# Regrouping the second half of batch 0's attention, and copying the second head group's keys in two parts

## The chip, the cores and the metric

The kernel runs on one core of a Trainium2 chip. The metric is the device time of one execution in microseconds (us), smaller is better. TensorE (PE in the profile, PEld its weight loads), VectorE (DVE), ScalarE (ACT) and GpSimd (POOL) each run their own list of instructions in order; SyncE (SP) only issues transfers. They meet through semaphores.

## The reference

Sigmoid attention over 8 batches, 12 heads, 448 positions and head size 64, followed by a gated feed-forward layer (ReGLU) on the 3584 tokens, model width 768, inner width 1536:

```python
scores = scale * np.matmul(q, k.transpose(0, 1, 3, 2)) - np.log(S)
attn = 1.0 / (1.0 + np.exp(-scores))
x = np.matmul(attn, v)                # then heads are put side by side: 3584 x 768
out = (np.maximum(x @ w_gate, 0.0) * (x @ w_val)) @ w_out
```

## The kernel before

Every instruction stands where the code puts it: the order on each engine is written by hand. The work of a batch goes through these steps.

- **Transposes.** `pe_transposes` (L195) turns the keys or queries of a group of four heads, chunk by chunk (7 chunks of 64 positions), with TensorE (L201) into a PSUM bank `trt`, and one VectorE copy (L206) brings them to `qkT` in SBUF. Keys and queries each take 14 transposes for all 7 chunks.
- **Scores and sigmoid.** In batch 0 the queries are handled in two parts, chunks 0 to 3 (256 columns) and 4 to 6 (192 columns); `FirstSlot` (L263) is one group (three groups) with one part of the queries, so there are six slots: 0 to 2 for the first part, 3 to 5 for the second. A slot has four units: units 0 to 2 hold two key chunks (8 score products, L232, four of them side by side in the array as 64x64 tiles), unit 3 one (4 products). A unit writes a tile of the pool `pairp`, which has two buffers (L69), and one sigmoid on ScalarE (L187) reads it into a `PT` tile. So a unit's products must wait until the sigmoid of the unit before last has read its buffer.
- **Value product.** `pv` (L242) multiplies all pieces of a slot by the values (28 products, L250, 64x64 tiles) into two PSUM banks, and two VectorE instructions (L184) scale them into `xT`.
- **Feed-forward unit.** `gv` (L304) makes, for 128 of the 1536 inner columns, 6 gate products and 6 value products (L309, full 128x128 weights); one instruction takes the maximum with 0 (on VectorE, L320, for the first part of batch 0; on ScalarE, L318, otherwise) and VectorE multiplies (L327). `ffn_mix(n)` (L651) runs the next n of these units. Their banks, those of `trt`, of `pv` and of `keep_warm` are given out in a ring of four (`bank`, L76).
- **Output.** The products with `w_out` follow from batch 2 on, in a form that saves multiplications.

`keep_warm` (L172) issues products of zeros. Loads are issued by GpSimd (L110 to L148) in a fixed order: keys, queries, values, then the weights in pieces of two to three units.

The order of batch 0 is a loop over the six slots and four units (L704); the dictionary `after` (L683) says what follows the unit (slot, unit): the transposes of later groups between slots 0 and 3, the value product of slot i about one slot later, and feed-forward units (first part, inner blocks 0 to 5, pushed at L669) between units of slots 3 to 5. `slots[5].pv()` (L709) ends batch 0's attention; the first call for batch 1 is L780, which transposes batch 1's first group and runs a feed-forward unit of the second part.

Of the kernel before, what the change touches and what calls it, by code (L numbers as in the profile page):

```python
# [17 lines left out]
def kernel(  # L18
# [17 lines left out]
    NCH = S // 64  # L36
# [3 lines left out]
    QCUT = 4  # L40
# [40 lines left out]
    def bank16(name):  # L81
        return bank(name, (P, 1024), FP16)
# [38 lines left out]
    KCUT = 4  # L121
# [50 lines left out]
    def keep_warm(count):  # L172
        ps = bank("warm_ps")
        for _ in range(count):
            nc.tensor.matmul(ps[:, 0:S], zeros[:, 0:P], zeros[:], start=True, stop=True)  # L175
# [14 lines left out]
    def qkT_of(b, g):  # L190
        if (b, g) not in qkT_tiles:
            qkT_tiles[(b, g)] = qkTp.tile([P, TW, P], FP16, tag="qkT", name="qkT")
        return qkT_tiles[(b, g)]

    def pe_transposes(b, g, ti, c0=0, c1=NCH):  # L195
        t16 = in_tiles[b][ti]
        qkT = qkT_of(b, g)
        trt = bank16("trt")
        for c in range(c0, c1):
            for h in range(2):  # L200
                nc.tensor.transpose(  # L201
                    trt[64 * h : 64 * h + 64, c * P : (c + 1) * P],
                    t16[:, 2 * g + h, c * D : (c + 1) * D],
                    ident[:],
                )
        nc.vector.tensor_copy(  # L206
            qkT[:, ti * NCH + c0 : ti * NCH + c1, :].rearrange("p c x -> p (c x)"),
            trt[:, c0 * P : c1 * P],
        )
# [437 lines left out]
    def push_first(half, fs, act_relu=True):  # L647
        c0, c1 = HALVES[half]
        push_gv(0, 64 * c0, 64 * (c1 - c0), fs, act_relu)

    def ffn_mix(count, hooks=()):  # L651
        hooks = list(hooks)
        for left in range(count, -1, -1):
            while hooks and hooks[0][0] >= left:
                hooks.pop(0)[1]()
            if left:
                gv_queue.popleft()()
# [10 lines left out]
    slots = [FirstSlot(half * NG + g, g, half) for half in range(2) for g in range(NG)]  # L668
# [2 lines left out]
        for g in range(1, NG):  # L671
            pe_transposes(0, g, 1, QCUT, NCH)

    def pv_then_ffn(i):
        slots[i].pv()
        ffn_mix(1)

    def ffn_then_pv(i):
        ffn_mix(1)
        slots[i].pv()  # L680


    after = {  # L683
        (0, 0): lambda: pe_transposes(0, 0, 0, KCUT, NCH),
        (0, 1): lambda: keep_warm(2),
        (0, 2): lambda: pe_transposes(0, 1, 0),
        (0, 3): lambda: pe_transposes(0, 1, 1, 0, QCUT),
        (1, 0): lambda: keep_warm(2),
        (1, 1): lambda: pe_transposes(0, 2, 0),
        (1, 2): lambda: pe_transposes(0, 2, 1, 0, QCUT),  # L690
# [5 lines left out]
        (3, 1): slots[2].pv,  # L696
        (3, 2): second_queries,
        (3, 3): lambda: ffn_mix(1),
        (4, 1): lambda: ffn_then_pv(3),
        (4, 3): lambda: ffn_mix(2),  # L700
        (5, 1): lambda: pv_then_ffn(4),
        (5, 3): lambda: ffn_mix(1),
    }
    for i, slot in enumerate(slots):  # L704
        for u in range(4):
            slot.unit(u)
            if (i, u) in after:
                after[(i, u)]()
    slots[5].pv()  # L709
    push_first(1, range(0, 6))  # L710
    for f0 in range(6, 12, 2):
        for half in range(2):
# [188 lines left out]
```

## Time and profile before

| what | value |
|---|---|
| median of 3 runs | 393.63 us (393.59 to 393.73) |
| profiled execution: its time | 393.45 us |
| profiled execution: span from first to last instruction | 391.7 us |
| granted TensorE clock | 1.00 |
| TensorE busy in 5.00 to 10.90 us | 5.37 us |
| TensorE, ScalarE busy in 10.90 to 17.70 us | 6.54, 6.71 us |
| TensorE, ScalarE, VectorE busy in 20.97 to 33.45 us | 12.48, 5.74, 7.64 us |

The span leaves 1.75 us of the execution's own time outside. In the page, a group line gives a line of the kernel, an engine, an operation, the tiles written and read, and how often it runs; the timeline gives the start, the duration and the form of instructions, with neighbours of one kind merged; the chain of waits goes back from the last instruction to whatever released each step. A product's duration includes its way through the array, so the rows of neighbouring products overlap, and TensorE can appear busy while nothing new can start: the distance between starts tells more than the duration.

### The profile page before, as it was taken

Reading aid. Unit: us, or ns where it says so; the run is one execution under the profiler, and the core shown is the slowest. Engines: PE = TensorE matmul, PEld = TensorE weight load, DVE = VectorE, ACT = ScalarE, POOL = GpSimd, SP = SyncE. Lnnn points to the kernel's source line nnn. Section 1 sums busy time; section 2 is a strip of 40 time slices with the busy share of each in tenths; the row PEclk is TensorE's granted clock in tenths of the full one; section 3 lists DMA queues with packets and bytes.
Section 4 is the critical chain, followed back from the end, with each engine's and each line's share of the span. In section 5 each row is a group of like instructions: output and inputs, shape, how many; then the busy total and the mean of one; then the engine's idle time right before and its main releaser. Section 6 shows DMA issues by size and latency. Waiting matters only on the chain.

```text
span 391.7 us, 8761 instructions
## 1 busy us (share of the span) xinstructions
PE 385.1 (98%) x3488; PEld 215.2 (55%) x3488; DVE 282.9 (72%) x556; ACT 226.7 (58%) x480; POOL 49.5 (13%) x73
## 2 busy tenths in 40 slices
PE   8999999999999999999999999999999999999996
PEld 4678786445455545454555554545455555555653
DVE  2464344358388789999757789999967788999563
ACT  4956778784877755555547774545477244333322
POOL 9634310500030300003000300000000000000000
PEclk9999999999999999999999999999999999999999
DMA  9999999998899892225945695133012330000335
GB/s 151 198 200 204 204 202 139 151 203 143 181 164 196 162 216 35 47 49 72 178 99 130 122 196 102 34 48 60 4 30 53 82 80 2 0 1 2 80 87 157
DMA packets 68953, 43.69 MB, mean 112 GB/s; under 512 B 35888, under 2 KB 65584, under 8 KB 68912
## 3 DMA queue, kind: packets, MB, share of 16 engines
q0 software_dynamic: 30736, 23.33, 39.6%
q1 hardware_dynamic: 37664, 19.24, 24.2%
q10 hardware_dynamic: 512, 0.56, 0.5%
q8 instruction: 27, 0.44, 0.4%
q14 instruction: 14, 0.11, 0.1%
HBM read 47.19 MB, written 11.01 MB: 149 GB/s over the span
## 4 chain that ended last, share of the span: by engine, by line
PE 95%; ACT 3%; DVE 1%; issue 0%; ACTq 0%
PE u L385 33%; PE g L385 16%; PE y L385 10%; PE qk_ps L232 9%; PE g_ps L309 8%; PE pv_ps L250 7%; PE v_ps L309 7%; ACT PT L187 2%; PE ya L346 1%; PE warm_ps L175 1%; PE trt L201 1%; PE yb L346 1%; DVE xT L184 0%; DVE qkT L206 0%; DVE S L376 0%
## 5 line engine op out<-in xcount | busy, mean ns | idle before, releaser
L187 ACT ACTIVATE PT<-qk_ps 128x448 f16<-128x448 f32 (+3 forms) x318 | 150.9, 589 | 76.2 <-PE qk_ps L232 76.1
L385 PEld LDWEIGHTS <-S 128*128 128x128 f16 x558 | 54.6, 98 | 45.5 <-issue 0.9
L597 DVE TENSOR_TENSOR gsb<-g,gsb 128x448 f32<-128x448 f32 x72 | 42.9, 625 | 10.4 <-PE g L385 10.0
L232 PE MATMUL qk_ps<-qkT 64*64 64x448 f16 (+2 forms) x756 | 47.4, 335 | 0.8 <-DVE qkT L206 0.5
L385 PEld LDWEIGHTS <-hT 128*128 128x128 f16 x306 | 28.6, 98 | 22.4 <-issue 5.0
L327 DVE TENSOR_TENSOR hT<-gate_sb,v_ps 128x256 f16<-128x256 f32 (+2 forms) x36 | 16.2, 465 | 34.0 <-ACT gate_sb L318 18.0
L593 ACT COPY gsb<-u 128x448 f32<-128x448 f32 x48 | 25.6, 558 | 24.0 <-PE u L385 22.9
L436 ACT ACTIVATE ysb<-u 128x384 f32<-128x384 f32 x31 | 15.3, 492 | 39.4 <-PE u L385 35.2
L184 DVE TENSOR_SCALAR xT<-pv_ps 128x448 f16<-128x448 f32 (+2 forms) x53 | 27.9, 566 | 13.1 <-PE pv_ps L250 12.2
L250 PE MATMUL pv_ps<-PT,v 64*64 64x448 f16 (+2 forms) x756 | 36.6, 329 | 0.0
L309 PE MATMUL g_ps<-xT,wg 128*128 128x256 f16 (+2 forms) x216 | 33.5, 291 | 0.1
L309 PE MATMUL v_ps<-xT,wv 128*128 128x256 f16 (+2 forms) x216 | 33.3, 290 | 0.0
L385 PEld LDWEIGHTS <-wg 128*128 128x128 f16 x216 | 20.2, 98 | 21.8 <-issue 4.3
L385 PEld LDWEIGHTS <-wv 128*128 128x128 f16 x216 | 21.1, 98 | 19.7
L232 PEld LDWEIGHTS <-qkT 64*64 64x64 f16 x756 | 17.9, 105 | 22.0 <-issue 13.8
L454 DVE SCALAR_TENSOR_TENSOR ysb<-y,ysb 128x384 f32<-128x384 f32 x28 | 15.6, 556 | 17.7 <-PE y L385 10.2
L250 PEld LDWEIGHTS <-v 64*64 64x64 f16 x756 | 21.7, 107 | 10.8 <-issue 0.9
L385 PE MATMUL u<-T,hT 128*128 128x384 f16 x138 | 26.2, 326 | 0.0
L309 PEld LDWEIGHTS <-wg 128*128 128x128 f16 x216 | 18.5, 98 | 11.7 <-issue 5.1
L110 POOL DMA_DIRECT2D k<-in_k_dram x14 | 10.9, 776 | 109.2 <-DVE rel L215 102.8
L309 PEld LDWEIGHTS <-wv 128*128 128x128 f16 x216 | 20.2, 98 | 7.4
L385 PE MATMUL u<-xT,wg 128*128 128x448 f16 x108 | 23.5, 354 | 0.0
(76 smaller groups left out, 531.7 us busy)
## 6 DMA issues: line engine op xcount, KB each, us to landing
out_dram<-ysb SPq DMA_DIRECT2D x52, 192.0 KB, 2.9
k<-in_k_dram POOLq DMA_DIRECT2D x5, 672.0 KB, 11.7
q<-in_q_dram POOLq DMA_DIRECT2D x5, 672.0 KB, 14.4
v<-in_v_dram POOLq DMA_DIRECT2D x8, 336.0 KB, 14.5
v<-in_v_dram POOLq DMA_DIRECT2D x16, 168.0 KB, 13.9
k<-in_k_dram POOLq DMA_DIRECT2D x8, 224.0 KB, 11.9
wo<-in_moe_w_out_dram POOLq DMA_DIRECT2D x1, 1536.0 KB, 11.1
q<-in_q_dram POOLq DMA_DIRECT2D x6, 224.0 KB, 12.2
```

The source lines that it names most:

```text
L110: nc.gpsimd.dma_start(t16[:, xs, cs], rows_of(src, b)[:, xs, cs])
L184: nc.vector.tensor_scalar(out=xT, in0=src, scalar1=XSCALE, scalar2=None, op0=AOP.mult)
L187: nc.scalar.activation(PT_ap, ps_ap, AF.Sigmoid, bias=sig_bias, scale=qk_scale)
L232: nc.tensor.matmul(out_of(hh)[o : o + 64, :], qkT[rows, c, cols], qkT[rows, NCH + c0 : NCH + c1, cols], start=True, stop=True, tile_positi ...
L250: nc.tensor.matmul(ps[hh][64 * r : 64 * r + 64, 0:qn], v16[rows, 2 * g + hh, c * D : (c + 1) * D], pieces[c][rows, hh, :], start=(c == 0), ...
L309: nc.tensor.matmul(ps[-1][:, 0:qn], wt[:, dc, f * P : (f + 1) * P], xT_tiles[b][:, dc, q0 : q0 + qn], start=(dc == 0), stop=(dc == NDC - 1),)
L327: nc.vector.tensor_tensor(out=hT_tiles[g][:, f, o : o + qn], in0=gate_sb[:, 0:qn], in1=ps[1][:, 0:qn], op=AOP.mult,)
L385: nc.tensor.matmul(ps[:, 0:n], A[:, k_, :], W[:, k_, :], start=(first and k_ == 0), stop=(k_ == kn - 1), skip_group_check=True,)
L436: nc.scalar.activation(o, ps[:, 0:HM], AF.Copy, scale=OUT_SCALE)
L454: nc.vector.scalar_tensor_tensor(out=o, in0=ps[:, 0:HM], scalar=OUT_SCALE, in1=o, op0=AOP.mult, op1=AOP.add)
L593: by(gs[u][i][:], ps[u][:, 0:S])
L597: nc.vector.tensor_tensor(out=gs[u][i][:], in0=ps[u][:, 0:S], in1=gs[u][i][:], op=AOP.add)
```

## The change

Two edits in the dictionary of batch 0; no instruction other than one VectorE copy is added or taken away.

1. The keys of the second group (g = 1) are transposed in two parts, chunks 0 to 3 with a copy of 512 elements a partition and chunks 4 to 6 with one of 384, where one copy of 896 stood. After unit 2 of slot 0 come the first part of the keys and the queries' chunks 0 to 3 (8 and 8 transposes); the second part of the keys (6) follows unit 3.
2. Slots 4 and 5 no longer have a feed-forward unit between their units: unit 0, unit 1, the value product of the slot before, unit 2 and unit 3 stand together, and two feed-forward units follow. The value product of slot 5, which stood at the end, is put ahead of the last of the six feed-forward units.

```diff
-    def pv_then_ffn(i):
-        slots[i].pv()
-        ffn_mix(1)
+    def first_of_second_group():
+        pe_transposes(0, 1, 0, 0, KCUT)
+        pe_transposes(0, 1, 1, 0, QCUT)
+
+    def last_value_product():
+        ffn_mix(2)
+        slots[5].pv()
+        ffn_mix(1)
-
-    def ffn_then_pv(i):
-        ffn_mix(1)
-        slots[i].pv()
...
-        (0, 2): lambda: pe_transposes(0, 1, 0),
-        (0, 3): lambda: pe_transposes(0, 1, 1, 0, QCUT),
+        (0, 2): first_of_second_group,
+        (0, 3): lambda: pe_transposes(0, 1, 0, KCUT, NCH),
...
-        (4, 1): lambda: ffn_then_pv(3),
+        (4, 1): slots[3].pv,
         (4, 3): lambda: ffn_mix(2),
-        (5, 1): lambda: pv_then_ffn(4),
-        (5, 3): lambda: ffn_mix(1),
+        (5, 1): slots[4].pv,
+        (5, 3): last_value_product,
...
-    slots[5].pv()
```

With u for a unit, P for a value product, F for a feed-forward unit and T for batch 1's transposes, TensorE's order from slot 4 on:

```
before  4u0 4u1 F P3 4u2 4u3 F F 5u0 5u1 P4 F 5u2 5u3 F P5 T
after   4u0 4u1 P3 4u2 4u3 F F 5u0 5u1 P4 5u2 5u3 F F P5 F T
```

## Prediction

> **What bounds the kernel now.** I read the page's engine lines first: TensorE is busy for 98% of the span. Then the chain of waits from 8.6 us on, which tells where the start of the kernel is set:
>
> ```profile
> 8.77 0.53 PE trt L201 x14
> 9.30 0.02 issue
> 9.33 0.62 DVE qkT L206
> 9.95 0.01 issue
> 9.97 0.44 DVE qkT L206
> 10.40 0.04 issue
> 10.45 0.44 PE qk_ps L232 x8
> 10.89 0.02 issue
> 10.91 3.35 ACT PT L187 x4
> 14.26 0.02 issue
> 14.28 3.35 ACT PT L187 x4
> 17.63 0.04 issue
> 17.67 0.36 PE qk_ps L232 x8
> ```
>
> Columns: start, length, who. Up to 10.45 us the two copies of the second group set the pace, then ScalarE's sigmoids without a hole until 17.63, and from 17.67 on the chain has nothing but TensorE for 36 us. So a gain ahead of 17.67 counts only if ScalarE gets it, and behind it each idle stretch of TensorE is lost time. The third view is TensorE's timeline in the stretch that the second edit reorders:
>
> ```profile
> 20.97 0.52 PE L232 MATMUL qk_ps<-qkT 64*64 64x192 f16 x16
> 21.43 0.83 PE L309 MATMUL g_ps<-xT,wg 128*128 128x256 f16 x6
> 22.09 0.82 PE L309 MATMUL v_ps<-xT,wv 128*128 128x256 f16 x6
> 22.84 0.77 PE L250 MATMUL pv_ps<-PT,v 64*64 64x192 f16 x28
> 23.44 0.42 PE L232 MATMUL qk_ps<-qkT 64*64 64x192 f16 x12
> ```
>
> and ScalarE's beside it, one sigmoid a line:
>
> ```profile
> 21.44 0.81 ACT L187 ACTIVATE PT<-qk_ps 128x768 f16<-128x768 f32 x1 [1.17 <-PE qk_ps L232]
> 22.15 0.81 ACT L187 ACTIVATE PT<-qk_ps 128x768 f16<-128x768 f32 x1
> ```
>
> To see: units 0 and 1 of slot 4 start at 20.97; their sigmoids end at 22.25 and 22.96. Units 2 and 3 need the buffers these two read. Today they come at 23.44, because a feed-forward unit and a value product stand between: the wait is there, and hidden.
>
> **Edit 1, the keys in two parts.** Eight transposes take 0.41 and fourteen 0.58 us (rows of the third group, 12.47 and 11.62), so six more cost 0.17. The first key copy can start at 9.33 - 0.17 = 9.16. A copy of 512 takes 0.43 (two in 0.85 at 5.68): it ends at 9.59. The queries' eight transposes follow 8 x 0.028 = 0.23 behind the keys', so their data are there at 9.39 and the second copy runs 9.59 to 10.01, where it ended at 10.39. Keys and queries have landed: the transfers issued at 2.29 and 3.00 took 4.9 and 4.8 us.
>
> Slot 1's unit 0 could start at 10.05 for 10.45. But its buffer is read by the sigmoid of slot 0's unit 2, 9.11 + 1.03 = 10.14, and 0.05 later the products start (13.82 after 13.76 one slot on): 10.19. From products to sigmoid it is 0.46 today (10.45 to 10.91), so 10.65, and ScalarE is free at 10.01 + 0.62 = 10.63. **ScalarE's hole of 0.28 shrinks to 0.02: -0.26 us**, and since its line then has no hole until 17.63, all of it reaches 17.67. The second part's six transposes take the place of the queries' eight, and its copy (0.36, the 384 row at 7.57) runs 10.01 to 10.37, while its first reader, slot 1's unit 2, stands at 12.13. VectorE works 0.17 us more, into idle time (1.85 us ahead of the copy at 12.24). The ring gives out one bank more; its reader of four turns ago is the copy that ended at 7.93. The term lies between -0.28, the whole hole, and 0, if another wait fills it; a loss would need the third copy to hold slot 1's unit 2, and it has 1.8 us of margin.
>
> What is late next: the first unit F starts at 19.30 for 19.56. Its value weights, issued at 9.72, land 9.8 later, at 19.5, and are read at 20.11 - 0.26 = 19.85. That margin of 0.3 holds. Later weights have more, since in the new order unit F number 2 comes 2 us later. GpSimd's and SyncE's lists keep their order, and no transfer moves past another.
>
> **Edit 2, what goes.** Changing between 64x64 and 128x128 products costs TensorE time. An F (a feed-forward unit) that another F follows lasts 1.32 from start to start (23.79 to 25.11), one that a value product follows 1.41 (21.43 to 22.84); the starts unrounded differ by 0.095. **A change is 0.095 us.** From slot 4's unit 0 to the F behind batch 1's transposes (20.97 to 32.36) there are 10 changes today and 7 after. Three fewer: **-0.29 us**.
>
> **Edit 2, what comes.** The new order puts units 2 and 3 right behind the value product. TensorE takes its list in order, so the two F queued behind them wait too, and behind these the next slot. Counting from unit 0's start at 20.97:
>
> - Units 0 and 1 with a value product last 1.03 up to the next F (26.52 to 27.55), less the change 0.095: TensorE is at unit 2 at 21.91. Its buffer is free when unit 0's sigmoid ends, 22.25, plus 0.05: 22.30. Idle 0.39.
> - Unit 2 takes two groups of four, 0.083 each (28.96 to 29.34 is three groups, the start 0.025 and a change): TensorE is at unit 3 at 22.47. Its buffer is free at 22.96 + 0.05 = 23.01. Idle 0.54.
> - Unit 3 to F is 0.21 (19.35 to 19.56): F at 23.22 instead of 22.29.
>
> That is **0.93 to 0.96 us idle in each of the two slots**; slot 5 stands the same way, since its ScalarE line is free when it begins (2.6 us of F lie between). I take 0.95. Units 2 and 3 have no cheaper way out: ScalarE issues its sigmoids 0.71 apart (21.44, 22.15) whatever TensorE does.
>
> **Sum.** 2 x 0.95 - 0.29 = +1.61. By pieces: each slot's attention has 1.50 today (0.46 + 0.095 + 0.95 in slot 4) and 2.25 after (20.97 to 23.22), which is 2 x 0.75, and slot 5's value product ahead of an F adds one change, 0.095: +1.59; with the starts unrounded it is +1.57, which I take. With edit 1: 1.57 - 0.26 = **+1.31 us**. Behind it, batch 1's first score products are reached 1.3 us later, with all inputs ready (its keys and queries landed at 28.8 and 29.9; the copies at 32.15 are no longer queued behind the scaling of slot 5's value product). The profiled execution would go from 393.45 to 394.76 (span 391.7 to 393.0); the median stands 0.18 above that execution, so 393.63 + 1.31 = **394.9 us**. About 0.2% (0.8 us) is what a measurement of this kernel can tell from no change.
>
> **A rule that speaks against the change.** After TensorE's 0.52 us of idle time before 10.45, the next pair of zero products still took 0.55 us, as before it (7.80 and 10.79), with the granted clock at 1.00; so one such hole did not slow it. The Trainium skill, TensorE: Matmul & The Clock Gate, section "A second HAM failure mode: psum-queue depth-cycling", says that short idle times between groups while PSUM buffers are cycled can throw the array back to half clock. The new order makes four holes of that size in 6 us. By the row this costs nothing, by the rule perhaps one window of 3.4 us at half clock, an estimate of 1.7 us from that page.
>
> **The rivals.**
>
> - *A, not slower: units 2 and 3 don't wait.* The mechanism is ScalarE's sigmoid of unit 0 ending before TensorE reaches unit 2, 0.94 us after the slot's start; the point is a sigmoid of 0.42 us. Then the sum is -0.29 - 0.26 = -0.55: 393.1 us. For it: TensorE shows no hole in this stretch today, and slot 3 passes its value product without one at 18.6. Against it: the rows give 0.81, and slot 3's unit 1 was itself held 0.27 us for its buffer (17.40 to 17.67).
> - *B, later waits take the lateness up.* TensorE waits once more behind batch 0's end, 0.68 us for VectorE at 298.57, and the chain goes over ScalarE for 0.54 at 53.77. If both were independent of TensorE: 394.9 - 0.68 - 0.23 = 394.0 (0.23 is what starts lost at 54.35). Against it: both wait for engines that work on TensorE's own results, so they move with it.
> - *C, edit 1 gives nothing,* a landing or a copy taking the hole's place: +1.57, 395.2.
> - *D, the clock falls back.* The trace has half-rate products only in the first 6 us (ten zero products in 3.92 us at 1.16, 0.37 apart, against two in 0.55 later, 0.20 apart), so the price is between 0 and 2.9 us (half of 1.16 to 6.9), 394.9 to 397.8; the nearest row, the hole at 10.45, says 0, and a case of its own begins above 395.4.
>
> **How the numbers follow.** Forecast 0.71, C 0.12, B 0.07, A 0.06, D 0.04. The range 394.4 to 395.4 takes in the forecast with 0.2 either way for the idle time (two slots, 0.1 each), and C: 0.83. Slower by over 0.2% (above 394.42): forecast, C, D, 0.87. Within: B and most of A, 0.11. Faster: 0.02.
>
> **What would show it.** ScalarE's row at 10.91 moves to 10.65 and the hole before it goes. In slots 4 and 5 the score products of units 2 and 3 stand apart, about 1.33 and 2.04 us after unit 0, released by ScalarE; the chain gets ScalarE pieces between 21 and 28 us where it has TensorE alone now. The transposes of batch 1 start at 32.7 for 31.45 and everything behind is 1.3 us later. If units 2 and 3 follow the value product without a hole, or the sigmoids are shorter, the forecast is wrong.

## The result, and the profile after

| | before | after |
|---|---|---|
| median | 393.61 us (393.39 to 393.76, 8 runs) | 394.84 us (394.35 to 395.49, 8 runs) |
| profiled execution: time | 393.45 us | 395.12 us |
| profiled execution: span | 391.7 us | 393.3 us |
| batch 1's first transposes start | 31.45 us | 32.83 us |

The change makes the kernel slower: the medians differ by 1.23 us, and the ratio is 1.0029, 95% interval 1.002 to 1.0039 (0.8 to 1.5 us). The forecast was 394.9.

The page of after first, engines and granted clock:

```profile
PE 385.6 (98%) x3488; PEld 215.6 (55%) x3488; DVE 283.1 (72%) x557; ACT 226.8 (58%) x480; POOL 49.5 (13%) x73
PEclk9999999999999999999999999999999999999999
```

VectorE has one instruction more, everything else the same number, and no slice of the span shows a lower clock. The busy time of TensorE is 98% here as before, and tells nothing of the 1.6 us that the span grew by. The chain of waits of after does (start, length, who):

```profile
8.38 2.32 ACT PT L187 x3
10.70 0.02 issue
10.72 3.35 ACT PT L187 x4
...
17.48 0.36 PE qk_ps L232 x8
...
21.30 0.49 PE pv_ps L250 x23
21.80 0.57 issue
22.37 0.32 PE pv_ps L250 x5
...
26.92 0.81 ACT PT L187
...
27.78 0.28 PE qk_ps L232 x4
```

Two things are to be seen. The copies of the second group have left the chain, and ScalarE leads from 8.38 to 17.44 without a hole: edit 1 does what it says, and TensorE takes over at 17.48 for 17.67. Behind 21 us two pieces have come in that before did not have: a ScalarE piece in slot 5, which was forecast, and an "issue" piece of 0.57 us in the middle of slot 4's value product, which was not. TensorE's timeline of after shows the same two places (the bracket gives the idle time before the row and what ended it):

```profile
20.78 0.53 PE L232 MATMUL qk_ps<-qkT 64*64 64x192 f16 x16
21.13 0.67 PE L250 MATMUL pv_ps<-PT,v 64*64 64x192 f16 x23
22.37 0.32 PE L250 MATMUL pv_ps<-PT,v 64*64 64x192 f16 x5 [0.57 <-issue]
...
23.02 0.83 PE L309 MATMUL g_ps<-xT,wg 128*128 128x256 f16 x6
...
25.74 0.53 PE L232 MATMUL qk_ps<-qkT 64*64 64x192 f16 x16
...
27.07 0.36 PE L232 MATMUL qk_ps<-qkT 64*64 64x192 f16 x8 [0.23 <-ACT PT L187]
27.78 0.28 PE L232 MATMUL qk_ps<-qkT 64*64 64x192 f16 x4 [0.34 <-ACT PT L187]
27.98 0.83 PE L309 MATMUL g_ps<-xT,wg 128*128 128x256 f16 x6
```

From unit 0 to the next feed-forward unit it is 23.02 - 20.78 = 2.24 us in slot 4 and 27.98 - 25.74 = 2.24 in slot 5, where the forecast had 2.25 for each. In slot 5 units 2 and 3 stand 1.33 and 2.04 us after unit 0, each released by ScalarE, to the hundredth as forecast. In slot 4 the time is the same and the place is another: the value product itself stops behind its 23rd product.

Along the program, after against before: slot 4's unit 0 -0.19 us, batch 1's first transposes +1.37, the same until 127 us, where the first score products of a batch wait for a DMA transpose and start 0.16 us later than at before's pace (+1.54 from there on), and +1.6 at the end.

### The profile page after: what moved, and what is told of

Its sections match the earlier page's. It is cut to its first block, busy times and chain, and to the rows that moved or that the text cites. A ratio compares the mean times of both kernels' runs of the same rounds, so it can differ in the third digit from the quotient of the medians.

```text
span 393.3 us, 8762 instructions
## 1 busy us (share of the span) xinstructions
PE 385.6 (98%) x3488; PEld 215.6 (55%) x3488; DVE 283.1 (72%) x557; ACT 226.8 (58%) x480; POOL 49.5 (13%) x73
## 4 chain that ended last, share of the span: by engine, by line
PE 92%; ACT 4%; DMA 1%; DVE 1%; issue 0%; ACTq 0%
PE u L385 32%; PE g L385 16%; PE y L385 9%; PE qk_ps L232 9%; PE g_ps L309 8%; PE pv_ps L250 8%; PE v_ps L309 7%; ACT PT L187 3%; DMA qkT<-rel 1%; PE ya L346 1%; PE warm_ps L175 1%; PE trt L201 1%; PE yb L346 1%; DVE xT L184 0%; DVE S L376 0%
## 5 line engine op out<-in xcount | busy, mean ns | idle before, releaser
L232 PE MATMUL qk_ps<-qkT 64*64 64x448 f16 (+2 forms) x756 | 47.8, 336 | 1.3 <-ACT PT L187 0.9
L309 PE MATMUL g_ps<-xT,wg 128*128 128x256 f16 (+2 forms) x216 | 33.5, 291 | 0.1
L309 PE MATMUL v_ps<-xT,wv 128*128 128x256 f16 (+2 forms) x216 | 33.3, 290 | 0.0
L385 PEld LDWEIGHTS <-wg 128*128 128x128 f16 x216 | 20.2, 98 | 21.8 <-issue 4.3
L232 PEld LDWEIGHTS <-qkT 64*64 64x64 f16 x756 | 18.2, 106 | 22.8 <-issue 14.5
L250 PEld LDWEIGHTS <-v 64*64 64x64 f16 x756 | 21.8, 107 | 11.4 <-issue 1.5
L385 PE MATMUL u<-T,hT 128*128 128x384 f16 x138 | 26.3, 326 | 0.0
L309 PEld LDWEIGHTS <-wg 128*128 128x128 f16 x216 | 18.6, 98 | 11.4 <-issue 5.1
L309 PEld LDWEIGHTS <-wv 128*128 128x128 f16 x216 | 20.2, 98 | 7.4
```

The costliest lines, as they stand in the source:

```text
L232: nc.tensor.matmul(out_of(hh)[o : o + 64, :], qkT[rows, c, cols], qkT[rows, NCH + c0 : NCH + c1, cols], start=True, stop=True, tile_positi ...
L250: nc.tensor.matmul(ps[hh][64 * r : 64 * r + 64, 0:qn], v16[rows, 2 * g + hh, c * D : (c + 1) * D], pieces[c][rows, hh, :], start=(c == 0), ...
L309: nc.tensor.matmul(ps[-1][:, 0:qn], wt[:, dc, f * P : (f + 1) * P], xT_tiles[b][:, dc, q0 : q0 + qn], start=(dc == 0), stop=(dc == NDC - 1),)
L385: nc.tensor.matmul(ps[:, 0:n], A[:, k_, :], W[:, k_, :], start=(first and k_ == 0), stop=(k_ == kn - 1), skip_group_check=True,)
```

## The experiments

Times are medians, each against runs of the kernel before taken beside it, with the ratio's 95% interval. In the traces the start of slot 0 moves by up to 0.6 us from one execution to the next, and it is the earlier the sooner the record of the full clock begins (4.6 to 7.0 us); places are therefore given as "relative", from slot 0's first score product. Batch 1's first score product stands at 26.63 relative in before and 27.97 in after.

**Edit 1 alone.**

```diff
...
-        (0, 2): lambda: pe_transposes(0, 1, 0),
-        (0, 3): lambda: pe_transposes(0, 1, 1, 0, QCUT),
+        (0, 2): first_of_second_group,
+        (0, 3): lambda: pe_transposes(0, 1, 0, KCUT, NCH),
```

> The kernel before with edit 1 alone (the second group's keys in two parts). Theory: the hole of 0.28 us in front of ScalarE's row at 10.91 shrinks to about 0.02 and all of it reaches the end: 393.61 - 0.26 = 393.35 us. Rival (the hole's place is taken by another wait, or ScalarE's gain is lost behind 17.67): 393.6 us.

Measured: 393.69 against 393.68, ratio 1.0002 (0.9993 to 1.0011). By itself the edit shows no gain. In the trace its 0.26 us are there in slot 1 and in slot 4 (each 0.26 earlier, relative) and gone at batch 1 (26.64 relative). TensorE's timeline of this kernel shows where, and its list of waits says for what (engine, line, releaser: us in total, times, longest):

```profile
27.06 0.83 PE L309 MATMUL g_ps<-xT,wg 128*128 128x256 f16 x6
27.98 0.83 PE L309 MATMUL v_ps<-xT,wv 128*128 128x256 f16 x6
```

```profile
PEld L309 <- DMA wv<-in_moe_w_val_dram: 0.4, 1, 0.4
```

Gate to value products takes 0.66 us elsewhere and 0.92 here: the value weights of inner blocks 4 and 5 land at 27.93. The DMA engines are busy for 90% or more of this stretch (every slice from 9 to 30 us shows 9 in the DMA row), so an earlier reader only waits longer. How much it waits changes with the execution: in before the same weights landed at 27.56, 0.65 us ahead of their reader, and in the second trace of before (the last experiment) at 27.92, only 0.06 ahead. This trace also loses 0.32 us at 126 us to a DMA transpose.

**Edit 2 alone.**

```diff
...
-        (4, 1): lambda: ffn_then_pv(3),
+        (4, 1): slots[3].pv,
         (4, 3): lambda: ffn_mix(2),
-        (5, 1): lambda: pv_then_ffn(4),
-        (5, 3): lambda: ffn_mix(1),
+        (5, 1): slots[4].pv,
+        (5, 3): last_value_product,
...
-    slots[5].pv()
```

> The kernel before with edit 2 alone (slots 4 and 5 unbroken, slot 5's value product ahead of the last feed-forward unit). Theory: two slots with units 2 and 3 held for ScalarE, 2 x 0.95 us idle, three changes of the array's form fewer: 393.61 + 1.57 = 395.2 us, with the holes in front of units 2 and 3. Rival (the loss comes from the two edits together, for example a transfer that is reached too early): between 393.6 and 394.5 us.

Measured: 394.79 against 393.68, ratio 1.0031 (1.0019 to 1.0044): +1.11 us (0.75 to 1.73) for a theory of +1.57; in the trace batch 1 stands 1.7 us later, relative. Edit 2 alone loses as much as the whole change, within the intervals. TensorE's timeline:

```profile
20.81 0.52 PE L232 MATMUL qk_ps<-qkT 64*64 64x192 f16 x16
...
22.64 0.32 PE L250 MATMUL pv_ps<-PT,v 64*64 64x192 f16 x5 [0.82 <-issue]
...
23.15 0.83 PE L309 MATMUL g_ps<-xT,wg 128*128 128x256 f16 x6
```

Slot 4 lasts 2.34 us to its feed-forward unit, 0.1 more than the sigmoids ask for, and the hole is again behind the 23rd product. No semaphore ends it: "issue" means that the profile shows nothing that TensorE waited for.

**After, with short sigmoids in slots 4 and 5.**

```diff
             n = qn * len(cs)
-            sigmoid(PT[:, :, 0:n], ps[:, :, 0:n])
+            m = qn if self.number > 3 else n
+            if m < n:
+                nc.vector.memset(PT[:, :, m:n], 0.0)
+            sigmoid(PT[:, :, 0:m], ps[:, :, 0:m])
```

> The changed kernel, but in slots 4 and 5 the sigmoids of units 0 to 2 take only the first of their two chunks, and VectorE sets the other half of the tile to zero: that part of the attention is left out, the products all stay. Theory (units 2 and 3 wait for the sigmoids of units 0 and 1): a sigmoid of 0.49 instead of 0.81 us lets unit 2 start 1.01 and unit 3 1.41 us after unit 0, and the next feed-forward unit 1.62 instead of 2.24: 0.62 less in each slot, 394.84 - 1.24 = 393.6 us. Rival (TensorE's holes come from its own instruction supply or the clock, not from ScalarE): 394.8 us.

Measured: 393.88 against 393.68, ratio 1.0011 (1.0002 to 1.002); 0.96 us under after. TensorE's timeline, slot 4 and slot 5 (L309 of the other kernels is L312 here):

```profile
20.39 0.53 PE L232 MATMUL qk_ps<-qkT 64*64 64x192 f16 x16
...
21.86 0.32 PE L250 MATMUL pv_ps<-PT,v 64*64 64x192 f16 x5 [0.45 <-issue]
...
22.36 0.83 PE L312 MATMUL g_ps<-xT,wg 128*128 128x256 f16 x6
...
25.09 0.53 PE L232 MATMUL qk_ps<-qkT 64*64 64x192 f16 x16
...
26.10 0.66 PE L232 MATMUL qk_ps<-qkT 64*64 64x192 f16 x12
26.69 0.83 PE L312 MATMUL g_ps<-xT,wg 128*128 128x256 f16 x6
```

Slot 5 falls from 2.24 to 1.60 us and its ScalarE holes are gone: there the sigmoids were the cause. They still set the pace, since units 2 and 3 start at 26.10 and 26.48, each 0.05 us after a sigmoid's end (26.05 and 26.43). Slot 4 falls only to 1.97, because the hole behind the 23rd product stays. So slot 4 has two limits that end close together.

**Slot 4 alone regrouped.**

```diff
-        (4, 1): lambda: ffn_then_pv(3),
-        (4, 3): lambda: ffn_mix(2),
+        (4, 1): slots[3].pv,
+        (4, 3): lambda: ffn_mix(3),
```

> The kernel before with slot 4 alone unbroken (its feed-forward unit stands behind unit 3, so three follow there); slot 5 as before. Theory: half of the regrouping's cost, 2.25 us for 1.50 in slot 4: 393.61 + 0.75 = 394.35 us. Rival (only slot 5, or the place of the last value product, costs): 393.6 us.

Measured: 394.08 against 393.68, ratio 1.0011 (1.0002 to 1.002). The trace has the hole at its longest, 1.04 us, with slot 4 starting early (20.59) and needing 2.57 us to its feed-forward unit:

```profile
22.66 0.32 PE L250 MATMUL pv_ps<-PT,v 64*64 64x192 f16 x5 [1.04 <-issue]
```

The end of the hole doesn't follow the start of slot 4: 22.37 in after (slot 4 from 20.78), 22.64 in edit 2 alone (20.81), 22.66 here (20.59), 21.86 with short sigmoids (20.39).

**After, with four zero products fewer ahead of slot 4.**

```diff
-        (1, 3): lambda: keep_warm(2),
-        (2, 0): lambda: keep_warm(2),
```

> The changed kernel without the four zero products that follow unit 3 of slot 1 and unit 0 of slot 2. In all four kernels with slot 4 unbroken so far TensorE stopped behind the same product, number 351 of its list, which is the 23rd of slot 4's value product, about 1.5 us after a packet of the instruction queue had ended. If TensorE's list arrives in blocks and the hole is the wait for the next one, it stands again behind product 351, now the 27th of the value product. If the hole belongs to the value product (its pieces or banks), it stands behind the 23rd again. The time tells little: 394.8 us by both.

Measured: 395.36 against 393.85, ratio 1.0042 (1.0028 to 1.0056). TensorE's timeline:

```profile
20.73 0.75 PE L250 MATMUL pv_ps<-PT,v 64*64 64x192 f16 x27
22.41 0.24 PE L250 MATMUL pv_ps<-PT,v 64*64 64x192 f16 x1 [0.93 <-issue]
```

Four products fewer ahead, and the hole stands four products later, behind the 27th. It belongs to a place in TensorE's list, behind its 351st product, and not to a tile or a buffer. The page's row of the instruction queue gives packets, MB and the share of the DMA engines:

```profile
q8 instruction: 27, 0.44, 0.4%
```

That is some 16 KB for each packet, and in each of the five kernels with this hole (after, edit 2 alone and the last three above) one packet ends 1.46 to 1.65 us before the hole does. In before, TensorE reaches product 351 at 23.04, 1.73 us after the packet's end at 21.31: no hole, by a margin of 0.1 to 0.3 us. The median is 0.5 us above the forecast: slot 4 lasts 2.45 us here for 2.24 in after, and score products at 100 and 127 us start 0.26 and 0.10 us later than at before's pace, behind DMA transposes.

**Slot 5 alone regrouped.**

```diff
-        (5, 1): lambda: pv_then_ffn(4),
-        (5, 3): lambda: ffn_mix(1),
+        (5, 1): slots[4].pv,
+        (5, 3): lambda: ffn_mix(2),
```

> The kernel before with slot 5 alone unbroken (its feed-forward unit stands behind unit 3, two there); slot 4 as before. Theory: ScalarE's two holes alone, without a hole of TensorE's list, F 2.24 us after unit 0, and 2.24 for 1.50: 393.68 + 0.74 = 394.4 us. Rival (the slot's cost was that of the list's blocks): 393.7 us.

Measured: 394.2 against 393.85, ratio 1.001 (1.0001 to 1.0019). The trace has the forecast's two holes and nothing else in slot 5. The first row below is slot 4's value product, which is that of before:

```profile
22.85 0.91 PE L250 MATMUL pv_ps<-PT,v 64*64 64x192 f16 x28
...
28.00 0.36 PE L232 MATMUL qk_ps<-qkT 64*64 64x192 f16 x8 [0.23 <-ACT PT L187]
28.70 0.28 PE L232 MATMUL qk_ps<-qkT 64*64 64x192 f16 x4 [0.34 <-ACT PT L187]
28.91 0.83 PE L309 MATMUL g_ps<-xT,wg 128*128 128x256 f16 x6
```

Slot 5's unit 0 starts at 26.66, so it is 2.25 us to the feed-forward unit; and from slot 5's unit 0 to batch 1's first score product 7.67 us for 6.93: +0.74, as expected. The value product of slot 4 takes 0.91 us for 0.77 in before: product 352 starts 0.14 us behind product 351, 1.60 us after a packet's end (21.59). So the list can hold TensorE without any change ahead of that place; no gap shows, because the row of the product before lasts 0.24 us. The medians of this and of slot 4 alone (+0.35 and +0.40) are about half of the +0.75 that each was expected to cost, which lies at the upper edge of both intervals, and lower than the traces' local sums (+0.74 and +1.05). In both profiled executions the clock came up early (5.3 and 4.6 us for 6.7 in before), which starts slot 0 0.4 to 0.5 us sooner. Whether that is so in the timed runs is not shown, so the split of the 1.1 us between the slots stays open within the intervals (0.0 to 0.8 us each).

**Edit 1 with the value weights in smaller pieces.** Does edit 1 pay if its new wait is taken away?

```diff
-    load_gv(4, 6)
+    load_gv(4, 5)
+    load_gv(5, 6)
```

> Edit 1 alone, with the weights of inner blocks 4 and 5 loaded one block at a time (four transfers for two). Edit 1 alone gained 0.26 us up to slot 5 and lost it in front of the value half of block 4, whose weights landed at 27.93. Theory: the value weights of block 4 alone land about 1 us sooner, that wait goes, and edit 1's gain reaches the end: 393.68 - 0.26 = 393.4 us. Rival (the smaller transfers cost the saturated queue as much as they bring, or a later landing takes the place): 393.7 us.

Measured: 394.18 against 393.85, ratio 1.0013 (1.0004 to 1.0021). The value weights of block 4 now land at 26.09, the wait is gone, and batch 1 starts 0.25 us earlier than in before (26.38 relative). In this trace it is lost one batch on, as the chain of waits and TensorE's timeline show (L233 is the other kernels' L232):

```profile
54.31 8.58 DMA qkT<-rel
```

```profile
62.93 0.57 PE L233 MATMUL qk_ps<-qkT 64*64 64x448 f16 x8 [0.77 <-DMA qkT<-rel]
```

A DMA transpose of 8.58 us holds batch 2's first score products until 62.93, 0.84 us later than at before's pace. The median is 0.33 us above before, where 0.26 below was expected, so edit 1's gain isn't seen in the time of this kernel either.

**One feed-forward unit in every gap, on top of edit 1.** The opposite of edit 2: cover between units instead of grouping.

```diff
     def pv_then_ffn(i):
         slots[i].pv()
+        ffn_mix(2)
+
+    def transposes_then_pv():
+        pe_transposes(1, 0, 0)
+        pe_transposes(1, 0, 1)
+        slots[5].pv()
         ffn_mix(1)
...
-        (4, 3): lambda: ffn_mix(2),
+        (4, 3): lambda: ffn_mix(1),
...
-        (5, 3): lambda: ffn_mix(1),
+        (5, 3): transposes_then_pv,
...
-    slots[5].pv()
...
-    ffn_mix(1, [(1, lambda: both(1, 0))])
+    ffn_mix(1)
```

> Edit 1, and every place where a unit's products would wait for ScalarE keeps a feed-forward unit: slot 4 as before but one such unit behind it instead of two, two behind slot 4's value product, and batch 1's transposes between slot 5's unit 3 and its value product, so that they cover the sigmoids there; one feed-forward unit follows. Value half of inner block 4 comes 1.3 us later in the order, so its weights' landing holds nothing. Theory: ScalarE's hole goes (0.26) and one change of the array's form (0.095), with no hole of ScalarE's in slots 4 and 5: the first product of batch 1 stands 26.3 us after slot 0's first for 26.63 before, and the time is 0.35 below the kernel before. Rival (the next limit, TensorE's list or a landing, takes it back): no difference, the first product of batch 1 at 26.6.

Measured: 394.0 against 393.88, ratio 1.0004 (0.9996 to 1.0013): no difference, and batch 1's first score product stands at 27.13 relative, 0.5 us behind before, where 26.3 was expected. TensorE no longer waits for ScalarE in slots 4 and 5; it waits for the loads instead. TensorE's timeline, one of the two places:

```profile
29.99 0.58 PE L201 MATMUL trt<-ident,q 128*64 128x128 f16 x14 [0.34 <-DMA q<-in_q_dram]
```

The transposes wait for batch 1's queries, which land at 29.95, and ahead of slot 5's unit 2 the value products of inner block 4 waited for their weights (landed at 27.90): they start at 27.95, 0.95 us behind their gate products for 0.66 elsewhere. The expectation had them 1.3 us later in the order; they stand 21.47 relative, for 21.39 in before, so the landing that it excused is one of the two that hold TensorE.

**The kernel before once more,** as it is.

> The kernel before, unchanged, for a second trace and a second row of times. If the limits that took back the gain of edit 1 alone (landing of weights and keys, blocks of TensorE's list, the landing of transposes near 126 us) already stand close to the kernel before, this trace shows small holes at one or more of these places, and slot 0's first product at another time than 6.82 us; times from 393.1 to 394.6 us. If they don't, its TensorE has no hole behind 17.7 us that the first trace lacks.

Measured: 393.56 against 393.88, ratio 0.9996 (0.9987 to 1.0005). Its trace has batch 1's first score product at 26.67 relative (26.63 in the first), and at 62.25 batch 2's first score products start 0.31 us behind the product before, for 0.18 in the first trace; the chain of waits has their DMA transpose (7.88 us) there, which the first trace lacks. So such waits come and go without any change of the kernel, and the 0.16 us at 127 in after are no sure part of the change's price.

## Why the prediction was right, step by step

- **The bound.** Right: ScalarE up to slot 3, then TensorE, and the idle stretches of slots 4 and 5 in after are still there at the end (+1.37 us at batch 1, +1.6 in the span).
- **Edit 1, -0.26.** Right in its place: the hole of 0.28 us before the row at 10.91 is 0.02 now, the row starts at 10.72 (forecast 10.65; slot 0 began 0.03 later), and slot 4 stands 0.23 earlier, relative (0.26 with edit 1 alone). What failed, for this edit alone, is the step behind it, "Later weights have more", meaning margin: in the trace of edit 1 alone the weights of inner blocks 4 and 5 take all of it back. The prediction excused them by the new order, and in after this holds, since their first reader comes at 29.96, 1.8 us behind their landing (28.20): rival C is right for edit 1 alone, and for the change it is wrong as far as the trace of after shows, up to batch 1. The times of after and of edit 2 alone (1.0029 and 1.0031) don't show the 0.26; the traces differ at batch 1 by 0.32 (27.97 and 28.29 relative), of which 0.1 is the longer hole in slot 4 of edit 2 alone.
- **Edit 2, +1.57.** The sum is right for the two edits together: +1.34 at batch 1 in the trace of after for a forecast of 1.31 with edit 1, and +1.23 in the medians (the profiled execution took 395.12 us for 394.76, with 0.16 of the difference at 127 us). In slot 5 the mechanism is shown: the holes are where they were put, of the size they were given, and go with shorter sigmoids. In slot 4 the size was right and the mechanism only half: TensorE stops behind its 351st product until 22.37, and unit 3 then starts at 22.81, 0.05 behind unit 1's sigmoid (21.25 + 1.51 = 22.76), just when it would have started anyway. Two limits ended together, and that the list added nothing to the sum in this execution is luck: where the list was the later one it added 0.1 us (edit 2 alone), 0.2 (four zero products fewer) and 0.3 (slot 4 alone). The prediction had no term for the list, because before shows no hole there.
- **Changes of array form, -0.29.** Not tried by itself. The two slots' lengths contain it and agree to 0.01 us, in slot 4 partly by that luck.
- **Rival A, no wait:** fell. With sigmoids of 0.49 us slot 5 passes without an idle row, but its units 2 and 3 still start 0.05 us after a sigmoid's end, so the point of 0.42 us that the prediction gave was not reached by any run.
- **Rival B, later waits absorb it:** fell. VectorE's wait late in the program is 0.68 us in after as it was in before, 1.53 us later (300.10 for 298.57), and ScalarE's piece of 0.54 stands at 55.15 for 53.77. Both moved with TensorE.
- **Rival D, the clock:** not seen. The granted clock is full from 6.96 us almost to the end of the execution, for as long as in before (385.7 us), though three idle stretches of TensorE stand between 21.8 and 27.8 us. The rule cited from TensorE: Matmul & The Clock Gate would have cost 1.7 us by the estimate given with it; the runs here side with the row at 10.45, for holes up to 1.04 us.

## What to carry to other kernels

Two buffers in front of a slower reader need other work between their second and third writer, and the price of taking it away can be counted beforehand, from the reader's end to the next writer's start. A stall taken away early in a kernel pays only as far as the next input's landing, so list the landing of every later operand beside its reader's new time, not only the first. When an engine idles with no semaphore to blame, look whether the place is fixed in its instruction list: take a few instructions out ahead of it and see whether the hole moves by as many.

## What was not expected of the hardware

- **TensorE can run out of its list.** Between 21 and 23 us, while the DMA engines are busy in every slice, the part of the list behind product 351 could be used only 1.46 to 1.65 us after a packet's end, and TensorE stood for 0.45 to 1.04 us. That the late part of the list is the cause follows from the hole's move with four products fewer, and no kernel starts product 352 sooner than 1.46 us after that packet; that the packets' path through the busy DMA engines makes them late is only argued.
- The Trainium skill, Runtime: NRT & Kernel Launch, section "Instruction fetch mechanics", says that an engine's list is refilled in blocks of 16 KiB and that crossing a boundary is mostly hidden. The packets of some 16 KB agree with it, and so do the 26 others of the 27, behind which no hole of this kind is seen; the hole behind product 351, up to 1.04 us in a stretch full of loads, is the exception.
- **DMA transposes land unevenly.** The first transpose of batch 2 took 5.3 to 8.6 us from issue to landing, and 7.0 and 7.9 in the two traces of the unchanged kernel. Score products started 0.1 to 0.8 us later than at before's pace at 62, 100 or 126 us in some traces and not in others. With the clock's start this may make up the spread of about 1 us that the timed runs of one kernel have; that is not shown.
